# Dealing the MLP's products out between the small products of a chunked recurrence

## The chip, the cores and the metric

The kernel runs on one core of a Trainium2 chip. The metric is the device time of one execution in microseconds (us); lower is better. Five engines work side by side, each through its own instruction stream in order: TensorE (PE in the profile, PEld for its weight loads), VectorE (DVE), ScalarE (ACT), GpSimd (POOL) and the engine that issues transfers (SP). They wait for each other through semaphores. Products land in PSUM[...].

## The reference

Two stages. The first is a linear recurrence over 768 tokens for 4 batches of 8 heads, each with a 40x40 state:

```python
for t in range(S):
    y[:, :, t] = np.einsum('bhd,bhde->bhe', rt, state)
    Sa = np.einsum('bhde,bhe->bhd', state, at)
    state_decay = state * wt[:, :, None, :] - np.einsum('bhd,bhe->bhde', Sa, bt)
    state = state_decay + np.einsum('bhd,bhe->bhde', vt, kt)
```

The second is an MLP over the 3072 tokens, 320 to 1024 to 320 wide:

```python
h = x @ w_in
e = np.exp(h - h_max)
solu = h * (e / (np.sum(e) + 1e-09))
ln = (solu - mu) / np.sqrt(var + 1e-06) * g_ln
out = ln @ w_out
```

All is float32.

## The kernel before

**Tiling.** The sequence is cut into 12 chunks (rounds n) of 64 tokens. A step i handles one chunk for two of the four batches, so there are 24 steps, two to a round. Inside a step the recurrence becomes products of 64x64 blocks: two batches times eight heads make 16 products of 64x64 (or 64x40), issued as one group. Each of a group's 16 matmuls is float32 and appears in the profile as two records, so a group reads as x32. Full-size work stands beside it: transposes (four of 128x128 to a group) and the MLP, whose products are 128x512 (hidden layer `h`, six matmuls in two PSUM banks) and 128x320 (output `po`, eight matmuls in one bank).

**Parts.** Each piece of work is a Python generator that issues some instructions and yields; `turns` takes letters and resumes the part that a letter names.

- `front(i)` (f, g): logarithm of w (`lw`), its cumulated sums (`pcum`, `pcx`), scaled b and k on GpSimd, transposes of a and b, and the triangular matrix `nt`.
- `scatter`, `gather`: `nt` of a round goes through DRAM (`blk_dram`) to a layout with one matrix a partition (`blk`).
- `invert(n)` (I): a triangular inversion on VectorE of 30 pairs of small operations (L408, L410), an opening that waits for `blk` (L398) and a close (copy `ut` and stores to DRAM). `bring_inverse` loads the result back.
- `attend(i)` (a): transposes of k, v and r, score groups `psi` and `lamv`, then `px0`.
- `solve(i)` (s): two groups of 32x32 products, `py` and `pz`, that complete the inverse.
- `recurrence(i)` (r): decayed state `sm` (GpSimd, L513), `px`, `x0` (VectorE), `pu`, its transposes `psT` and `pnu`, the scores `lamu`, and the new state (`pst`, `tot`).
- `readout(i)` (y): `pyo` and the product with `exT`.
- `hidden(m)` (h) and `output(m)`: the MLP of step m = i - 6. `hidden` makes `h`, then the row maximum `nmax` (VectorE), `exp` into `e` (ScalarE), e times h in place (VectorE), and the statistics. `output` transposes the result (`plnT`, copied to `lnT` by ScalarE), multiplies by `w2` into `po`, and scales it into `osb` (ScalarE).
- `weights()` (W): narrows the MLP's weights piece by piece with VectorE, ScalarE and GpSimd (L163 to L174), and scales `w2` at its end (L238).

**Order.** The whole schedule is written by hand (`manual_schedule`): what the letters issue first stands first in each engine's queue. Steps 0, 1 to 5 and 6 to 23 use the strings FIRST, EARLY and STEADY (L684 to L686). After the string, a step calls `scatter`, the rest of the inversion (`steps(inv, ...)`), three weight pieces while i < 6, and in steady steps the whole of `output(m)`: eight transposes and eight products in a row (L740 to L741). In STEADY the products of `h` stand in two places: four of six matmuls behind `px` and `pcum`, two behind `pvT`. All small groups from `py` to `px0` follow one another. After step 23 a loop runs the last six `hidden` and `output` (L748 to L753).

**Buffers.** Small PSUM tiles of one bank (`bank`) rotate through two buffers, tiles of two banks (`duo`: all 64x64 groups) through two, and `h` has one of two banks. `e`, `lnT` and `osb` have one buffer each.

Of the kernel before, what the change touches and what calls it, by code (L numbers as in the profile page):

```python
# [17 lines left out]
P = 128  # L18
# [34 lines left out]
def kernel(  # L53
# [256 lines left out]
    def decay(i):  # L310
# [19 lines left out]
        for j in range(2):  # L330
            t = bank("pcx")
            for g in range(2):
# [3 lines left out]
                                 func=AF.Exp)  # L336

# [8 lines left out]
    def front(i):  # L346
# [8 lines left out]
        yield  # L355
        next(parts)
        yield
        next(parts, None)
# [76 lines left out]
    def attend(i):  # L435
# [6 lines left out]
        rT = d["rT"] = transposed("rT", given(i, "r"), "rT", 2)  # L442
        yield
        psi = d["psi"] = wide("psi")
        scores("psi", kT, d["aT"], psi)
        yield
# [59 lines left out]
    def recurrence(i):  # L506
# [15 lines left out]
        yield  # L522
        t = duo("pu")
# [13 lines left out]
        if ci:  # L537
            t = bank("psT")
            for c in range(2):
                for m in range(2):  # L540
                    at = (2 * c + m) * P
                    nc.tensor.transpose(out=t[:, at:at + P], in_=sm[:, c, 2 * m:2 * m + 2, :]
                                        .rearrange("q g d -> q (g d)"), identity=ident)
            sT = two.tile([P, 2, 2, P], FP32, tag="sT", name="sT", bufs=1)
            nc.scalar.copy(out=sT.rearrange("q c m e -> q (c m e)"), in_=t)
        yield
        t = bank("pnu")
        for g in range(G):
            nc.tensor.transpose(out=t[:, g * P:(g + 1) * P], in_=nuT[:, g, :], identity=ident)  # L549
        nc.scalar.copy(out=nu.rearrange("p h c -> p (h c)"), in_=t)  # L550
        yield
# [5 lines left out]
        scores("lamu", nuT, d["rT"], lamu)  # L557
        yield
# [49 lines left out]
    def hidden(i):  # L608
# [9 lines left out]
        part(0, 0)  # L618
        part(0, 1)
        yield  # L620
        part(1, 0)
        part(1, 1)
# [25 lines left out]
    def output(i):  # L648
# [7 lines left out]
        yield  # L656
        o = bank("po")
        for f in range(NF):
            nc.tensor.matmul(o[:, 0:DM], lhsT=lnT[:, f, :], rhs=w2[:, f, :], start=f == 0, stop=f == NF - 1)  # L659
        if s == 0:  # L660
            of_round[n]["osb"] = two.tile([P, 2, DM], FP32, tag="osb", name="osb", bufs=1)
        nc.scalar.activation(out=of_round[n]["osb"][:, s], in_=o[:, 0:DM], func=AF.Copy, scale=st[i]["rs"])  # L662
        yield
# [19 lines left out]

    FIRST = "r f r I a f a g a r r g f r f I s g y s I r a g a I f g a"  # L684
    EARLY = "r f I r a f a W a r r f r f I s W y s r W a a f a"
    STEADY = "r I f h r a f a h a r r h f r f s h y s r a a f a h h"  # L686
    front_of = {}

    def begin(i):
# [95 lines left out]
```

## Time and profile before

845.56 us, the median of 3 runs (839.35 to 847.56). The profiled execution spans 845.0 us.

| engine | busy us | share of the span | instructions |
|---|---|---|---|
| PE | 641.1 | 76% | 12281 |
| DVE | 462.4 | 55% | 1257 |
| ACT | 272.3 | 32% | 633 |
| POOL | 128.4 | 15% | 202 |

The costliest groups of instructions, with the mean time of one and the idle time of the engine just before them:

| line and operation | count | busy us | mean ns | idle before, us |
|---|---|---|---|---|
| L613 matmul h, 128x512 | 288 | 126.4 | 657 | 16.5 |
| L659 matmul po, 128x320 | 384 | 115.3 | 455 | 4.1 |
| L408, L410 inversion pairs on VectorE | 720 | 201.4 | 280 | 23.9 |
| L333 matmul pcx, 128x132 | 192 | 35.9 | 326 | 4.4 |
| L518 matmul px, 64x40 | 704 | 16.5 | 243 | 41.7 |
| L624 row maximum nmax | 24 | 29.4 | 1223 | 60.8 |

How to read them: a matmul counts as busy from its start to a modelled end, and neighbours overlap, so the rows for small groups show less than the time that they hold the engine. The idle column belongs to one engine; idle time of an engine that is not the bottleneck costs nothing. The `pu` groups, one to a step, mark the steps in time: step 0 begins at 64.5 us, step 1 at 102.4, step 6 at 268.5, step 19 at 642.7 and step 23 at 736.9.

### The profile page before, as it was taken

The numbers are of one execution on the slowest core, as the hardware profiler recorded it, in microseconds if no ns is written. First come the engines' busy times: TensorE is split into PE (matmuls) and PEld (weight loads), VectorE is DVE, ScalarE is ACT, GpSimd is POOL, SyncE is SP. The second block draws the span as 40 slices with busy tenths as digits, with TensorE's granted clock in tenths as the row PEclk, the third lists the DMA queues.
The fourth block names the chain that finished last, engine by engine and source line by source line (L and its number), as shares of the span: only waits on it lengthen the run. The fifth ranks groups of instructions, "written<-read, shape, count | busy, mean of one in ns | idle before, by whom it ended". The sixth has DMA issues, their size and how long they took to land.

```text
span 845.0 us, 28218 instructions
## 1 busy us (share of the span) xinstructions
PE 641.1 (76%) x12281; PEld 458.0 (54%) x12281; DVE 462.4 (55%) x1257; ACT 272.3 (32%) x633; POOL 128.4 (15%) x202
## 2 busy tenths in 40 slices
PE   5418365465477889888988988898888998978786
PEld 4316254354355666575667656665666666644344
DVE  2574375565538547467576585584675842342322
ACT  3113235344322333244234423432333332321211
POOL 3201124323301111111110111011110000000000
PEclk9659586696687998999899999999999999998988
DMA  7577445536504535425326346364213311010000
GB/s 113 92 126 114 120 89 111 122 61 108 108 1 82 94 56 88 86 50 99 75 58 90 67 78 108 66 99 78 50 31 75 76 36 44 5 35 0 16 16 16
DMA packets 269802, 59.99 MB, mean 71 GB/s; under 512 B 255464, under 2 KB 265328, under 8 KB 269680
## 3 DMA queue, kind: packets, MB, share of 16 engines
q1 hardware_dynamic: 269536, 57.98, 37.3%
q8 instruction: 96, 1.57, 0.8%
q10 hardware_dynamic: 144, 0.23, 0.1%
q14 instruction: 26, 0.21, 0.1%
HBM read 40.08 MB, written 13.37 MB: 63 GB/s over the span
## 4 chain that ended last, share of the span: by engine, by line
PE 51%; DVE 16%; issue 11%; ACT 6%; DMA 2%; POOL 1%; SPq 1%; ACTq 0%; DVEq 0%; POOLq 0%
PE h L613 11%; PE po L659 8%; DVE prod L408 4%; DVE u L410 4%; PE pyo L585 3%; PE pst L565 3%; PE plnT L654 2%; PE pcx L333 2%; DMA blk<-blk_dram 2%; PE pz L476 2%; PE pyo L502 2%; PE py L476 1%; PE pnu L549 1%; PE pu L529 1%; ACT rT L257 1%
## 5 line engine op out<-in xcount | busy, mean ns | idle before, releaser
L613 PE MATMUL h<-w_in,xT 128*128 128x512 f32 (+1 forms) x288 | 126.4, 657 | 16.5 <-DVE e L631 13.3
L659 PE MATMUL po<-w,lnT 128*128 128x320 f32 x384 | 115.3, 455 | 4.1 <-ACT lnT L655 4.1
L408 DVE TENSOR_TENSOR prod<-blk,u 128x30 f32<-128x30 f32 (+4 forms) x360 | 101.5, 282 | 11.5 <-DMA blk<-blk_dram 0.5
L410 DVE TENSOR_TENSOR u<-u,prod 128x30 f32<-128x30 f32 (+4 forms) x360 | 99.9, 278 | 12.4
L659 PEld LDWEIGHTS po<-w,lnT 128*128 128x128 f32 x384 | 75.0, 200 | 40.1 <-ACT lnT L655 8.8
L613 PEld LDWEIGHTS h<-w_in,xT 128*128 128x128 f32 (+1 forms) x288 | 42.7, 199 | 71.7 <-issue 71.4
L624 DVE TENSOR_REDUCE nmax<-h 128x1 f32<-128x1024 f32 x24 | 29.4, 1223 | 60.8 <-PE h L613 60.8
L572 POOL TENSOR_TENSOR st<-tot,kx 128x320 f32<-128x320 f32 x20 | 15.0, 749 | 282.0 <-DVE tot L571 282.0
L662 ACT ACTIVATE osb<-po,rs 128x320 f32<-128x320 f32 x24 | 12.7, 528 | 112.9 <-PE po L659 66.2
L518 PE MATMUL px<-sm,kx 64*64 64x40 f32 x704 | 16.5, 243 | 41.7 <-POOL sm L513 41.7
L631 DVE TENSOR_TENSOR e<-h,e 128x1024 f32<-128x1024 f32 x24 | 29.3, 1219 | 27.2 <-ACT e L628 27.2
L366 DVE TENSOR_TENSOR kx<-paT,kx 128x512 f32<-128x512 f32 x24 | 16.5, 690 | 48.7 <-PE paT L365 48.6
L646 POOL TENSOR_TENSOR rs<-c,mhalf 128x1 f32<-128x1 f32 x24 | 13.2, 549 | 193.7 <-DVE c L645 193.7
L518 PEld LDWEIGHTS px<-sm,kx 64*64 64x64 f32 x704 | 13.8, 149 | 49.8 <-POOL sm L513 42.2
L323 PE MATMUL pcum<-lw,cst 128*128 128x320 f32 x48 | 24.4, 597 | 21.5 <-ACT lw L319 21.5
L655 ACT COPY lnT<-plnT 128x512 f32<-128x512 f32 x48 | 26.3, 588 | 43.2 <-PE plnT L654 43.1
L534 ACT ACTIVATE nuT<-pu 128x128 f32<-128x128 f32 (+1 forms) x72 | 17.3, 313 | 70.4 <-PE pu L529 70.4
L460 ACT COPY x_own<-px 128x320 f32<-128x320 f32 x22 | 9.4, 426 | 94.0 <-PE px L454 94.0
L333 PE MATMUL pcx<-cst,lw 128*128 128x132 f32 x192 | 35.9, 326 | 4.4 <-ACT kT L257 4.2
L326 POOL TENSOR_TENSOR kx<-raw_b,inv 128x320 f32<-128x320 f32 x24 | 21.1, 880 | 97.1 <-ACT inv L324 84.0
L333 PEld LDWEIGHTS pcx<-cst,lw 128*128 128x128 f32 x192 | 30.4, 224 | 9.2 <-ACT kT L257 7.0
L520 DVE TENSOR_TENSOR x<-x_own,px 128x320 f32<-128x320 f32 x22 | 10.7, 486 | 43.1 <-PE px L518 26.1
(108 smaller groups left out, 1208.1 us busy)
## 6 DMA issues: line engine op xcount, KB each, us to landing
blk<-blk_dram SPq DMA_DIRECT2D x24, 256.0 KB
raw_w<-in_w_dram SPq DMA_DIRECT2D x24, 160.0 KB
raw_b<-in_b_dram SPq DMA_DIRECT2D x24, 160.0 KB
raw_a<-in_a_dram SPq DMA_DIRECT2D x24, 160.0 KB
raw_k<-in_k_dram SPq DMA_DIRECT2D x24, 160.0 KB
v<-in_v_dram SPq DMA_DIRECT2D x24, 160.0 KB
r<-in_r_dram SPq DMA_DIRECT2D x24, 160.0 KB
out_dram<-osb SPq DMA_DIRECT2D x24, 160.0 KB
```

Source lines behind the costliest of these rows:

```text
L333: nc.tensor.matmul(t[:, g * 132:g * 132 + 132], lhsT=pair(lw, 2 * j + g), rhs=cst[:, lo:lo + 132], start=True, stop=True)
L408: nc.vector.tensor_tensor(out=t, in0=nb[:, j:j + 1, j + 1:Q].to_broadcast([P, rows, m]), in1=u[:, 0:rows, j:j + 1].to_broadcast([P, rows, ...
L410: nc.vector.tensor_tensor(out=u[:, 0:rows, j + 1:Q], in0=u[:, 0:rows, j + 1:Q], in1=t, op=ALU.subtract)
L476: nc.tensor.matmul(t[quarter(out), c:c + Q], lhsT=lhs(p, g), rhs=rhs(p, g), start=True, stop=True)
L518: nc.tensor.matmul(t[half(c ^ p), p, g * D:g * D + D], lhsT=d["aT"][half(p), g, half(c)], rhs=sm[half(p), c, g, 0:D], start=True, stop=True)
L565: nc.tensor.matmul(t[half(p), c, g * D:g * D + D], lhsT=kb[half(c), j, 2 * g + p, :], rhs=x[half(c), G * p + g, 0:D], start=j == 0 and g = ...
L585: nc.tensor.matmul(t[half(p), c, g * L:g * L + L], lhsT=kb[half(c), j, 2 * g + p, :], rhs=lam[half(c), h % 2, h // 2, :], start=i < 2 and ...
L613: nc.tensor.matmul(h[:, j * 512:j * 512 + 512], lhsT=of_round[i // 2]["xT"][rows, kt, i % 2 * P:i % 2 * P + P], rhs=w_in[rows, 4 if kt == ...
L624: nc.vector.tensor_reduce(out=nmax, in_=h, axis=AX.X, op=ALU.max, negate=True)
L631: nc.vector.tensor_tensor(out=q, in0=h, in1=e, op=ALU.mult)
L655: nc.scalar.copy(out=lnT[:, fs.start:fs.stop].rearrange("p f t -> p (f t)"), in_=t)
L659: nc.tensor.matmul(o[:, 0:DM], lhsT=lnT[:, f, :], rhs=w2[:, f, :], start=f == 0, stop=f == NF - 1)
```

## The change

The MLP's large products are dealt out between the groups of small products, and the MLP of a step is spread over two steps. The intent is that large and small products alternate on TensorE, with less work standing in a clump.

- `hidden` makes `h` in five passes (both short products, then each of the other four alone) in place of two.
- `output` yields between its two groups of transposes and after each two of its eight products, and it runs one step later, dealt out by the letter o. The statistics of `hidden` (letter b) run one step later too. `store` moves into `output`.
- `decay` yields between the two `pcx` halves; `attend` makes `rT` after `psi`; in `recurrence`, `psT` comes before `pu`, and `pnu` after `lamu`.
- The three order strings are new. In EARLY (now also for step 0), five weight pieces are spread through the step, with none behind the string. The inversion has 12 steps in an early string and 16 in a steady one; what is left of it at the end of an even step is issued there, and now ahead of `scatter`.
- The loop after step 23 follows the new division.

```diff
@@ decay, front
                                  func=AF.Exp)
+            yield
...
-        next(parts)
-        yield
-        next(parts, None)
+        for _ in range(2):
+            next(parts)
+            yield
+        next(parts)
@@ attend
-        rT = d["rT"] = transposed("rT", given(i, "r"), "rT", 2)
-        yield
         psi = d["psi"] = wide("psi")
         scores("psi", kT, d["aT"], psi)
+        yield
+        rT = d["rT"] = transposed("rT", given(i, "r"), "rT", 2)
         yield
@@ recurrence: ahead of pu
+        if ci:
+            t = bank("psT")
...
+            nc.scalar.copy(out=sT.rearrange("q c m e -> q (c m e)"), in_=t)
+        yield
         t = duo("pu")
@@ recurrence: behind pu
-        if ci:
-            t = bank("psT")
...
-        t = bank("pnu")
-        for g in range(G):
-            nc.tensor.transpose(out=t[:, g * P:(g + 1) * P], in_=nuT[:, g, :], identity=ident)
-        nc.scalar.copy(out=nu.rearrange("p h c -> p (h c)"), in_=t)
-        yield
...
         scores("lamu", nuT, d["rT"], lamu)
+        yield
+        t = bank("pnu")
+        for g in range(G):
+            nc.tensor.transpose(out=t[:, g * P:(g + 1) * P], in_=nuT[:, g, :], identity=ident)
+        nc.scalar.copy(out=nu.rearrange("p h c -> p (h c)"), in_=t)
         yield
@@ hidden
-        part(0, 0)
-        part(0, 1)
-        yield
-        part(1, 0)
-        part(1, 1)
+        for j in range(2):
+            for kt in range(2):
+                yield
+                part(j, kt)
@@ output
-        yield
+            yield
         o = bank("po")
...
+            if f % 2 and f < NF - 1:
+                yield
...
+        if s:
+            store(n)
@@ the order
-    FIRST = "r f r I a f a g a r r g f r f I s g y s I r a g a I f g a"
-    EARLY = "r f I r a f a W a r r f r f I s W y s r W a a f a"
-    STEADY = "r I f h r a f a h a r r h f r f s h y s r a a f a h h"
+    EARLY = ("r r f I W r a r r I W y r a f I W a s a f W a f s f W a f",
+             "r r f g I W r a r r I W y r a f g I W a s a f g W a f g s f g W a f g")
+    STEADY = "r r f b b I r o o a o r r I o y o r I o a f h a s a h f I a h f s h f h a f h h"
@@ the loop over the steps
-            turns(FIRST if i == 0 else EARLY if i < LAG else STEADY,
-                  dict(I=4 if i < LAG else 6 if i % 2 else 12), **parts)
+            turns(EARLY[len(js) - 1] if i < LAG else STEADY, dict(I=4), **parts)
             if i % 2:
                 load((i + 3) // 2, "v", "r")
                 repack(i // 2)
+            else:
+                steps(inv, 99)
             if js and js[-1] % 2:
                 scatter(js[-1] // 2)
-            steps(inv, 9 if i % 2 else 99)
-            if i < LAG:
-                steps(ws, 3)
-            if m >= 0:
-                steps(output(m), 2)
-                if m % 2:
-                    store(m // 2)
             begin(i + 1)
+            after, before = now, output(m) if m >= 0 else None
@@ the loop behind step 23
-            turns("h o h o h h h h", {}, h=hidden(m), o=before)
...
+            turns("h h o o h h b b h o o o o h h", {}, h=now, b=after, o=before)
+            after, before = now, output(m)
+        turns("b b o o o o o o", {}, b=after, o=before)
```

## The prediction

> **What bounds the kernel now.** I read the page first, then the busy time by stretch, then the waits of two stretches, then timelines of TensorE, VectorE and ScalarE. From the page (sections 1, 2, 3 and 4):
>
> ```profile
> span 845.0 us, 28218 instructions
> PE 641.1 (76%) x12281; PEld 458.0 (54%) x12281; DVE 462.4 (55%) x1257; ACT 272.3 (32%) x633; POOL 128.4 (15%) x202
> PEclk9659586696687998999899999999999999998988
> q8 instruction: 96, 1.57, 0.8%
> PE 51%; DVE 16%; issue 11%; ACT 6%; DMA 2%; POOL 1%; SPq 1%; ACTq 0%; DVEq 0%; POOLq 0%
> ```
>
> TensorE is the fullest engine, but idle for 204 us, and 11% of the chain is "issue", time in which it waits for nothing that the profile shows. The stages differ, so I cut the span at the starts of the `pu` products (one per step): steps 0; 1 to 4; 7 to 18; 19 to 22; 23 with the tail. The columns are stretch, length, busy time of PE, PEld, DVE, ACT and POOL with counts, granted clock, DMA share, GB/s.
>
> ```profile
> 64.50:102.40 37.90, 19.55 (x470) 15.19 (x469) 16.64 (x53) 11.17 (x28) 5.21 (x7) 0.73 0.58 111
> 102.40:230.70 128.30, 71.97 (x1909) 59.62 (x1908) 76.09 (x236) 52.55 (x143) 42.08 (x67) 0.73 0.51 103
> 298.70:642.70 344.00, 301.64 (x6265) 217.18 (x6264) 220.51 (x578) 121.08 (x274) 47.25 (x69) 0.97 0.41 74
> 642.70:736.90 94.20, 84.48 (x1829) 59.84 (x1828) 47.70 (x120) 32.17 (x72) 7.22 (x11) 0.98 0.21 42
> 736.90:845.00 108.10, 82.20 (x413) 46.42 (x412) 31.16 (x58) 20.90 (x40) 3.84 (x7) 0.89 0.06 16
> ```
>
> Early steps 1 to 4 take 32.1 us each and no engine is busy for more than 19.1; steady steps take 28.7 us with TensorE busy for 25.1. So the early steps are bound by a wait and the steady ones by TensorE. The early wait, from the waits of 102.4 to 230.7:
>
> ```profile
> PE px L518 <- POOL sm L513: 41.7, 4, 12.1
> ACT parts L165 <- DVE parts L163: 34.2, 21, 5.4
> POOL w L174 <- DVE parts L171: 33.6, 12, 7.6
> ```
>
> At each step's end stand nine or more steps of the inversion on VectorE and then three weight pieces; their last operation is on GpSimd (L174), and the next step's `sm` (L513) queues behind it there. TensorE waits 10.4 us per step. In a steady step, from TensorE's timeline:
>
> ```profile
> 454.19 0.69 PE L585 MATMUL pyo<-lamu,kx 64*64 64x64 f32 x32
> ...
> 458.40 0.60 PE L565 MATMUL pst<-nu,kx 64*64 64x40 f32 x27 [1.48 <-issue]
> ...
> 460.78 1.13 PE L274 MATMUL pnt<-kx,bT 64*64 64x64 f32 x32
> ```
>
> The gap falls inside a group that has already begun, after seven small groups in a row, and afterwards such a group takes 1.13 us, not 0.69: the clock has dropped. The packets of the instruction queue tell why: 1.57 MB in 96 packets is 16.4 KB each, and in this step they start at 446.39, 455.20, 459.88 and 463.25 us, 3.4 to 4.7 us apart once the small groups run. Over steps 6 to 22 such gaps add up to 29 us of TensorE's idle time.
>
> **What the Trainium skill says.** "Runtime: NRT & Kernel Launch", Instruction fetch mechanics: each engine's instructions are refilled in 16 KiB blocks of 256, and the cost is mostly hidden. The trace agrees on the block (16.4 KB), not on hidden: the 12,281 matmuls and as many weight loads make 96 such blocks, and a small group (64 instructions in 0.5 to 0.7 us) uses a block in 2.4 us, faster than 3.4 to 4.7. "TensorE: Matmul & The Clock Gate", Part 1: idle time of about a window (3.4 us) halves the clock. Here 1.5 us was enough (0.69 to 1.13). "TensorEngine Tiling (Array Packing)", Key Properties: changing the tiling mode drains the engine. The trace has four transposes in 0.44 us where more transposes follow (449.70 to 450.14) and in 0.59 where a group of 32x32 follows (452.92 to 453.51), so some 0.1 us a change. "PSUM — Partial Sum Buffer", Engine vs sequencer instructions: ScalarE, VectorE and GpSimd are strict FIFOs; all waits above agree.
>
> **The change, part by part.** It adds no arithmetic; matmuls, copies and transfers are the same in number. Everything is order.
>
> Early steps. Weight pieces go from 3 in the step and 3 at its end to 5 spread through it; the inversion takes 12 steps in turn, and even steps still end with a clump of 8 (7 short pairs of some 0.45 us, as at 407.15 to 407.64, and the 0.61 copy: 3.75 us). `sm` no longer stands behind a weight piece that follows a clump: the 10.4 us wait goes. What stays is a chain on VectorE. An even step (0 is the end of `nt` of the step before): `x0` 1.3; `pu` 2.6 to 3.7; four pairs and a piece on VectorE to 5; `lamu` 6.1; four pairs, a piece, `x`, `tot` 10.5; four pairs, a piece, `psi` 14.4; a piece, `lamv`, `kx`, a piece 17.4; then `bT`, `pnt`, `nt` 19.1 us. An odd step meets a new wait: the scatter now stands behind the clump and its stores: 3.75 + 1.7 (issue of the stores) + 1.8 (of four scatters) + 2.0 (landing, as from 43.71 to the gather at 45.74) + 3.8 (gather to VectorE's start: 3.6 to 4.2 in the trace) = 13.1 us, and VectorE stops at its first inversion step after `x0` (4.2) until then. Behind it stand 1.4 us of setup (416.04 to 417.43), three pairs 1.4 (417.43 to 418.83), a piece 0.8 and `lamu` 0.7 = 17.4; TensorE's `pyo` and all after it wait. The remaining 12.2 us are VectorE's, as in the even step: 29.6 us. Two pairs are 2 x (19.1 + 29.6) = 97.4, against 128.3: **minus 31**. Bounds: 27 us instead of 29.6 if the gather is early, 24 instead of 19.1 if GpSimd or the clock drags: minus 21 to minus 36. Step 5 (mean product, 6.3 us, in both): minus 1. Step 0: the gain-row product `pg` now stands before `pu` and waits for GpSimd to free the round's inputs, some 9 us, where 7.24 us were waited at the step's end; 5.87 us of waiting for `lw` go: minus 4, between plus 5 and minus 10.
>
> Steady steps. The densest stretches are now px0, pnt, px, psT, pcum, pu (280 instructions in some 5 us) and pyo to ppsi, in which 9 large products stand between the groups (about 256 in 5.2 us): slower than the fetch, so the "issue" gaps (29 us in steps 6 to 22, 1.7 a step) go, and with them the lost clock (3% of 25.1, 0.7 us). Mode changes rise from 11 to about 17: plus 0.4. Busy: 25.1 - 0.7 + 0.4 = 24.8. New waits, from 0 at the end of h's last pass: `nmax` 1.28, `exp` 2.5, its product 3.76 and `x0` 4.25, since VectorE runs `e` before `x0`; TensorE has px0, pnt, px, psT and pcum (3.0 us; pcum itself waits for `lw`, behind `exp` on ScalarE, to 3.0), so `pu` waits 1.3. pkT needs the bank of the first transposes, freed by ScalarE at 6.4: 0.45 with po. pcx needs po's bank, freed by `osb`: 0.25. Sum 26.8 on even steps. The 0.2 to 0.5 us waits for `lw`, `kT`, `rT` and `lnT` of before are replaced by these. On odd steps VectorE's queue has the gather's wait in it:
>
> ```profile
> 404.70 0.69 DVE L276 TENSOR_TENSOR nt<-pnt,cst 128x512 f32<-128x512 f32 x1 [0.40 <-PE pnt L274]
> ...
> 412.75 0.49 DVE L520 TENSOR_TENSOR x<-x_own,px 128x320 f32<-128x320 f32 x1 [2.43 <-ACT osb L662]
> 416.04 0.42 DVE L398 TENSOR_SCALAR u<-blk 64x512 f32<-64x512 f32 x1 [2.80 <-DMA blk<-blk_dram]
> ```
>
> Today that wait is hidden: `lamu` is needed 12 us after `px`, behind two stretches of h. After the change `nt` ends at 2.0, the data are there 2.0 + 4.3 + 3.8 = 10.1, setup, three pairs and `lamu` follow to 13.6, and `pyo` could have run at 10.6: plus 3.0 (1.5 to 5, and a cold clock may add 1). So 29.8, and a pair averages 28.3 against 28.7: **minus 5** for steps 7 to 18, from minus 30 (no new waits) to plus 25. Step 6 has no output product yet (5.6 us) and loses a 4.5 us wait, against 1.6 new: minus 8.5. Steps 19 to 22: 0, the same exchange.
>
> Tail. One more output product stands in step 23 and the exponent's chain there is bare: plus 9. The period of the last six stays: po's four parts still stand before the exponent, so on ScalarE
>
> ```profile
> 770.06 0.53 ACT L662 ACTIVATE osb<-po,rs 128x320 f32<-128x320 f32 x1 [5.46 <-issue]
> 770.49 1.11 ACT L628 ACTIVATE e<-h,nmax 128x1024 f32<-128x1024 f32 x1
> ```
>
> `osb`, which waits for po, still precedes `exp`, and TensorE's 3.2 us idle follows, with h at 4.69 instead of 3.04 us.
>
> Sum: -4 - 31 - 1 - 8.5 - 5 + 9 = -40.5: 845.5 to about 805; I say **806**.
>
> **Rivals.** (B) The gather lands early or the waits for `x0` and `lamu` overlap, and the steady stage keeps the whole of issue gaps and clock: 12 x 2.4 more = 29 less: **777**. For it: the gaps are real, and step 9 shows only 24.2 us of TensorE work (27.03 less 2.8 idle). Against: `lamu` follows `px` so soon now. (C) The early steps gain only 15, because the clump and its stores hold the gather longer, and odd steady steps wait 5 us: **840**, no change to speak of. (D) Slower: each steady step pays for `x0` and `lamu` in full and the idle time drops the clock (1.7 us each, as in the tail), 31.0 a step: plus 28, tail plus 9, early minus 20: **862**. For it: three strict queues are now chained in each step. Against: VectorE is busy for 18 of 28.7 us only.
>
> **How the numbers follow.** A 0.50 (790 to 825), B 0.25, C 0.11, D 0.14. Faster by over 1%: A, B and a little of C: 0.77; same 0.09; slower 0.14. The range 766 to 846 leaves out some of B's lower end and most of D.
>
> **What would show it.** Right: `px <- POOL sm` gone from the early waits, early pairs near 49 us; issue gaps in steady steps below 0.5 us; new rows `pu <- DVE x`, `pyo <- DVE lamu` (odd steps), `pcum <- ACT lw` near 1 us; tail unchanged. Wrong: issue gaps still there (then fetch is not what they are), `sm` still late, or a clock under 0.95 in the steady stage.

## The result, and the profile after

894.7 us (median of 4 runs, 891.7 to 899.8) against 846.6 for the kernel before beside it: ratio 1.059, 95% interval 1.050 to 1.068. Forecast were 806 us, with 766 to 846 as range. The change makes the kernel slower, by 48 us. The profiled execution (899.8 us) is the longest of the four.

The page's lines that answer to those shown of before (sections 1, 2, 3 and 4):

```profile
span 898.0 us, 28194 instructions
PE 663.6 (74%) x12281; PEld 464.5 (52%) x12281; DVE 464.2 (52%) x1257; ACT 272.1 (30%) x633; POOL 127.1 (14%) x202
PEclk9655758657656998999999999999999999887978
q8 instruction: 97, 1.59, 0.8%
PE 51%; DVE 16%; SPq 10%; DMA 9%; ACT 7%; issue 6%; POOL 0%; ACTq 0%; DVEq 0%; POOLq 0%
```

The arithmetic is the same (12,281 matmuls), but TensorE is busy for 22.5 us more on it. "issue" fell from 11% of the chain to 6%, as meant; but SyncE's queue went from 1% to 10% and the transfers from 2% to 9%. PEclk shows where: in slices 2 to 13 there are five fives and no nine, where the kernel before had two of each, and five of the last six are below nine again.

By the same stages, again cut at the starts of `pu` (step 0; 1 to 4; 7 to 18; 19 to 22; 23 with the tail):

```profile
82.90:107.50 24.60, 21.96 (x469) 18.30 (x469) 13.70 (x37) 12.27 (x32) 4.73 (x7) 0.68 0.19 63
107.50:256.80 149.30, 76.76 (x1915) 64.19 (x1914) 80.28 (x246) 47.97 (x133) 38.93 (x62) 0.69 0.39 79
326.80:671.00 344.20, 305.29 (x6264) 211.82 (x6264) 218.71 (x583) 122.02 (x274) 47.12 (x69) 0.97 0.42 77
671.00:772.20 101.20, 86.76 (x1826) 58.54 (x1826) 48.28 (x121) 32.55 (x72) 7.20 (x11) 0.96 0.22 43
772.20:898.00 125.80, 98.17 (x440) 55.18 (x440) 32.96 (x64) 22.40 (x42) 4.38 (x8) 0.83 0.06 14
```

| stage | before | after | difference | predicted |
|---|---|---|---|---|
| up to step 0's `pu` | 64.5 | 82.9 | +18.4 | |
| step 0 | 37.9 | 24.6 | -13.3 | with the row above: -4 |
| steps 1 to 4 | 128.3 | 149.3 | +21.0 | -31 |
| step 5 | 37.8 | 45.8 | +8.0 | -1 |
| step 6 | 30.2 | 24.2 | -6.0 | -8.5 |
| steps 7 to 18 | 344.0 | 344.2 | +0.2 | -5 |
| steps 19 to 22 | 94.2 | 101.2 | +7.0 | 0 |
| step 23, tail | 108.1 | 125.8 | +17.7 | +9 |

The early steps (up to step 6, plus 34) and the end (from step 19 on, plus 25) make it slower, not the steady steps. The waits of steps 1 to 4, first TensorE's, then VectorE's, then the fullest of ScalarE's (that one from 107.5 to 302.6, step 5 included); columns: who waits, for what, us in total, times, longest:

```profile
PE plamu L274 <- ACT nuT L546: 38.2, 4, 20.4
PE pbT L255 <- ACT tinvT L493: 14.0, 2, 7.5
PE pcx L333 <- ACT y_mid L490: 8.9, 4, 2.9
...
DVE parts L163 <- DMA bits<-in_moe_w_out_dram: 19.4, 2, 9.7
DVE u L400 <- DMA blk<-blk_dram: 18.2, 2, 9.2
...
ACT parts L165 <- DVE parts L163: 89.4, 16, 19.6
```

`px <- POOL sm` is gone, as predicted. But of the 72 us that TensorE now waits in these steps, 62 are for copies by ScalarE, and ScalarE stands in a weight piece (L165) for VectorE's part of it (L163), which stands behind either the gather of the inversion's blocks (`u`, odd steps) or the piece's own bits (even steps). (Not all inputs are float32: the two weight matrices of the MLP arrive as 64-bit numbers, `bits`, and a piece narrows a stretch of them.) Step 1 in order of time, on VectorE, ScalarE and TensorE:

```profile
124.65 0.42 DVE L400 TENSOR_SCALAR u<-blk 64x512 f32<-64x512 f32 x1 [9.17 <-DMA blk<-blk_dram]
127.40 0.29 DVE L163 TENSOR_SCALAR parts<-bits 128x256 int32<-128x256 int32 x1
127.73 0.51 ACT L165 ACTIVATE parts<-parts,ebias 128x256 int32<-128x256 int32 x1 [19.65 <-DVE parts L163]
128.77 0.70 ACT L546 ACTIVATE nuT<-pu 128x256 f32<-128x256 f32 x3
129.18 1.13 PE L274 MATMUL plamu<-rT,nuT 64*64 64x64 f32 x32 [20.37 <-ACT nuT L546]
```

One late transfer holds VectorE, VectorE holds ScalarE, ScalarE holds `nuT`, and TensorE idles 20.4 us; its next group takes 1.13 us, at a granted clock of 0.50. In step 2 it is SyncE's queue, a line of transfers to issue from 145.26 on (its first row and its last two), before VectorE's wait for bits that came last in it:

```profile
145.26 2.27 SPq L300 DMA_DIRECT2D v<-in_v_dram  x2
...
168.22 2.72 SPq L300 DMA_DIRECT2D raw_k<-in_k_dram  x2
171.05 6.50 SPq L213 DMA_DIRECT2D bits<-in_moe_w_out_dram  x5
...
174.78 0.24 DVE L163 TENSOR_SCALAR parts<-bits 128x160 int32<-128x160 int32 x1 [9.72 <-DMA bits<-in_moe_w_out_dram]
```

The Trainium skill ("Perfetto Trace Analysis", DMA Instruction — HWDGE (DVE, Sync)) says that a queue's sequencer is free for the next instruction only when the descriptors of the last are made. The trace agrees: 35 issues follow one another from 145.26 to 172.60, 0.78 us each on average and at most 0.11 us apart, and the first of the weights' fetches stood behind 32 of them. (The last row runs to 177.55 because its last two fetches wait, for 4.1 us together, until VectorE frees their buffers.)

The steady steps did what was predicted, but for step 7. TensorE's waits from 326.8 to 671:

```profile
PE pyo L587 <- DVE lamu L276: 18.1, 6, 5.1
PE pu L541 <- DVE x L522: 10.7, 13, 3.6
PE pcum L323 <- ACT lw L319: 4.5, 11, 0.4
...
PE pst L567 <- issue: 0.4, 1, 0.4
```

No gap for instructions is left (0.4 us in twelve steps), even steps take 26.4 (step 8: 27.1), odd ones 28.2 to 31.7, and step 7 takes 34.9.

### The profile page after: what moved, and what is told of

The parts are those of the page before. It is cut to its first block, busy times and chain, and to the rows that moved or that the text cites. A ratio compares the mean times of both kernels' runs of the same rounds, so it can differ in the third digit from the quotient of the medians.

```text
span 898.0 us, 28194 instructions
## 1 busy us (share of the span) xinstructions
PE 663.6 (74%) x12281; PEld 464.5 (52%) x12281; DVE 464.2 (52%) x1257; ACT 272.1 (30%) x633; POOL 127.1 (14%) x202
## 4 chain that ended last, share of the span: by engine, by line
PE 51%; DVE 16%; SPq 10%; DMA 9%; ACT 7%; issue 6%; POOL 0%; ACTq 0%; DVEq 0%; POOLq 0%
PE h L615 13%; PE po L660 10%; DMA blk<-blk_dram 4%; SPq L300 4%; DVE u L412 3%; DVE prod L410 3%; PE pyo L587 3%; PE pcx L333 3%; DVE nmax L625 2%; PE pst L567 2%; DMA blk_dram<-nt 2%; SPq L385 2%; ACT e L629 2%; DVE e L632 2%; PE plnT L655 2%
## 5 line engine op out<-in xcount | busy, mean ns | idle before, releaser
L615 PE MATMUL h<-w_in,xT 128*128 128x512 f32 (+1 forms) x288 | 137.1, 682 | 19.6 <-DVE e L632 16.5
L660 PE MATMUL po<-w,lnT 128*128 128x320 f32 x384 | 129.0, 471 | 0.1
L412 DVE TENSOR_TENSOR u<-u,prod 128x30 f32<-128x30 f32 (+4 forms) x360 | 109.0, 303 | 12.4
L274 PE MATMUL plamu<-rT,nuT 64*64 64x64 f32 x768 | 18.2, 241 | 48.8 <-ACT nuT L546 48.8
L333 PE MATMUL pcx<-cst,lw 128*128 128x132 f32 x192 | 34.6, 313 | 15.3 <-ACT y_mid L490 10.8
L333 PEld LDWEIGHTS pcx<-cst,lw 128*128 128x128 f32 x192 | 29.4, 212 | 27.0 <-ACT y_mid L490 15.9
L276 DVE TENSOR_TENSOR lamu<-plamu,cst 128x512 f32<-128x512 f32 x24 | 16.5, 689 | 50.3 <-PE plamu L274 50.3
L400 DVE TENSOR_SCALAR u<-blk 64x512 f32<-64x512 f32 x12 | 5.2, 431 | 71.9 <-DMA blk<-blk_dram 67.5
L541 PE MATMUL pu<-tinvT,x 64*64 64x64 f32 x768 | 20.2, 246 | 29.8 <-DVE x L522 19.4
L274 PEld LDWEIGHTS plamu<-rT,nuT 64*64 64x64 f32 x768 | 15.6, 153 | 50.0 <-ACT nuT L546 50.0
L647 POOL TENSOR_TENSOR rs<-c,mhalf 128x1 f32<-128x1 f32 x24 | 13.1, 548 | 194.6 <-DVE c L646 180.7
L165 ACT ACTIVATE parts<-parts,ebias 128x160 int32<-128x160 int32 (+1 forms) x26 | 11.9, 458 | 92.6 <-DVE parts L163 92.6
L656 ACT COPY lnT<-plnT 128x512 f32<-128x512 f32 x48 | 26.9, 603 | 41.7 <-PE plnT L655 41.6
L541 PEld LDWEIGHTS pu<-tinvT,x 64*64 64x64 f32 x768 | 16.8, 150 | 39.9 <-DVE x L522 27.3
```

The costliest lines, as they stand in the source:

```text
L274: nc.tensor.matmul(t[half(c ^ p * cross), p, g * L:(g + 1) * L], lhsT=lhs[half(p), g, half(c)], rhs=rhs[half(p), g, half(c)], start=True, ...
L333: nc.tensor.matmul(t[:, g * 132:g * 132 + 132], lhsT=pair(lw, 2 * j + g), rhs=cst[:, lo:lo + 132], start=True, stop=True)
L412: nc.vector.tensor_tensor(out=u[:, 0:rows, j + 1:Q], in0=u[:, 0:rows, j + 1:Q], in1=t, op=ALU.subtract)
L541: nc.tensor.matmul(t[half(z), c ^ p, h // 2 * L:h // 2 * L + L], lhsT=x0[half(c ^ p), h, :], rhs=d["tinvT"][half(c ^ p), p, h % G, :], sta ...
L615: nc.tensor.matmul(h[:, j * 512:j * 512 + 512], lhsT=of_round[i // 2]["xT"][rows, kt, i % 2 * P:i % 2 * P + P], rhs=w_in[rows, 4 if kt == ...
L656: nc.scalar.copy(out=lnT[:, fs.start:fs.stop].rearrange("p f t -> p (f t)"), in_=t)
```

## The experiments

All ratios are to the kernel before, with 95% intervals; "steps 1 to 4" is the time between the starts of `pu` in steps 1 and 5. It is read from one profiled execution of each kernel; kernels that have the same early steps agree in it within 1.5 us (149.3, 149.1 and 148.5; 134.0, 133.8 and 135.0; 128.3 and 127.2), so differences of 3 us or less say little.

**Which stages lose.** Two edits, each to the changed kernel: the early steps dealt out as before (`OLD` holds the strings of before, fitted to the new parts), and the tail's exponent ahead of the output product.

```diff
-            turns(EARLY[len(js) - 1] if i < LAG else STEADY, dict(I=4), **parts)
+            turns(OLD[len(js) - 1] if i < LAG else STEADY, dict(I=4), **parts)
...
-            else:
-                steps(inv, 99)
             if js and js[-1] % 2:
                 scatter(js[-1] // 2)
+            if i < LAG:
+                steps(inv, 9 if i % 2 else 99)
+                steps(ws, 3)
+            elif i % 2 == 0:
+                steps(inv, 99)
```

> Steps 0 to 5 run in the order of the kernel before (its strings, its clump of the inversion, three weight pieces at the step's end, scatter ahead of the clump); everything else is the changed kernel, the new order of psT, pnu and rT included. Theory A (the early strings are the loss): step 6 begins near 268 us as in the kernel before and not at 302.6, and the whole takes about 860 (855 to 868). Theory B (the new order of the parts themselves, psT ahead of pu and rT behind psi, costs the early steps): step 6 begins after 285 and the whole stays above 875.

849.2 us, ratio 1.005 (1.002 to 1.008): 46 us less, Theory A and more than it said; step 6 begins at 264.3. Steps 1 to 4 take 134.0 and wait for `sm` again (40.9 us), step 5, whose mean product moved into step 4, 24.2. Steps 7 to 18 take 334.1, 9.9 less than before. The edit does more there than its expectation says: in steady steps, too, the scatter stands ahead of the inversion's rest. Step 7, 34.9 in the changed kernel, takes 28.1 (below, the scatter's place alone gives 28.6).

```diff
-            turns("h h o o h h b b h o o o o h h", {}, h=now, b=after, o=before)
+            turns("h h o o h h b b h h o o o o h", {}, h=now, b=after, o=before)
```

> In the loop behind step 23 the exponent is issued ahead of the four parts of the output product, so that on ScalarE it no longer stands behind osb; nothing else. Theory A (the order of osb and exp on ScalarE makes the 3.1 us idle time of each round and the low clock after it): the round falls from 15.4 to about 10.5 us, six rounds, so 25 to 30 us less, about 867. Theory B (the maximum, exponent and product chain is longer than the output product anyway): 5 us less or nothing.

862.0 us, ratio 1.019 (1.013 to 1.026): Theory A. Step 23 and the tail fall from 125.8 to 92.0. ScalarE in a round of the changed kernel, then in one of this:

```profile
805.52 0.53 ACT L665 ACTIVATE osb<-po,rs 128x320 f32<-128x320 f32 x1 [6.47 <-PE po L660]
805.95 1.11 ACT L629 ACTIVATE e<-h,nmax 128x1024 f32<-128x1024 f32 x1
```

```profile
808.54 1.11 ACT L629 ACTIVATE e<-h,nmax 128x1024 f32<-128x1024 f32 x1 [3.15 <-DVE nmax L625]
...
811.71 0.53 ACT L665 ACTIVATE osb<-po,rs 128x320 f32<-128x320 f32 x1 [1.97 <-issue]
```

In the first `exp` waits behind `osb`, which waits for the whole of `po`; in the second it runs while TensorE computes `po`, and a round takes 9.9 us instead of 15.4 on average. The edit works on the kernel before as well:

```diff
-            turns("h o h o h h h h", {}, h=hidden(m), o=before)
+            turns("h o h h o h h h", {}, h=hidden(m), o=before)
```

> The kernel before with one edit in the tail: the exponent stands ahead of the output product and its osb. Theory A (the tail's idle 3.2 us a round and the cold clock after it are the kernel's own, not the change's, and five rounds each lose 4 to 5 us): 846 less 22 = 824 us (818 to 830). Rival B (the gain needs the four parts of the output product that the change made): less than 8 us, 838 to 847 us.

819.6 us, ratio 0.972 (0.963 to 0.981), the tail 84.0 for 108.1. So the idle time in a round is the kernel's own; the swap shortens five rounds here and six in the changed kernel. And the two losses add:

> The changed kernel with both edits that gained by themselves: steps 0 to 5 dealt out as before, and in the tail the exponent ahead of the output product's last parts. Theory A (the two losses lie in different stages and add): 849 less 34 = 815 us (808 to 822), step 6 begins near 264, the tail from the start of step 23 takes 92. Rival B (the tail's gain came out of work that the late early steps had pushed on): the tail gains 15 at most, 834 us (827 to 845).

817.1 us, ratio 0.964 (0.959 to 0.968), step 6 at 265.3.

**What the early steps lose to.** First with all weights ahead of the loop, so that no piece stands in the steps:

```diff
         ws, after, before = weights(), None, None
+        steps(ws, 99)
```

> All weight pieces are worked off ahead of step 0, so that none stands in the early strings; the whole is not comparable, the early steps are. Theory A (a weight piece's ScalarE part stands ahead of the recurrence's copies and hands VectorE's wait on to TensorE): the waits plamu on nuT, pbT on tinvT and pcx on y_mid fall under 1 us a step, and steps 1 to 4 take 95 to 110 us together in place of 149. Theory B (the gather blocks VectorE and lamu behind it, weights or not): odd steps stay at 33 us or more and TensorE waits over 10 us for lamu in each; only the even ones fall, to about 22, so steps 1 to 4 take 110 to 125.

877.1 us (a single run; the pieces' time is now ahead of step 0, which begins at 130.4). The stretch of steps 1 to 4, and TensorE's wait in it:

```profile
151.40:256.10 104.70, 62.96 (x1913) 52.84 (x1912) 65.25 (x186) 30.50 (x73) 15.37 (x21) 0.82 0.44 80
```

```profile
PE pyo L587 <- DVE lamu L276: 28.8, 4, 18.2
```

The sum, 104.7 us or 44.6 less, is Theory A's, and what is left is Theory B's: behind the gather TensorE waits for `lamu` 18.2 us in step 1 and 8.8 in step 3, where it had waited 20.4 and 10.6 for `nuT`. So in odd steps the late gather makes most of that wait, pieces or not; ScalarE's queue only gives it another name. Even steps fall from 37.7 and 37.1 to 21.1 and 20.8, odd ones from 41.2 and 33.3 to 35.5 and 27.4: some 16 us of an even step and 6 of an odd one are the pieces'. (The kernel before has pieces in these steps too; what its steps would take without them was not measured.) What of a piece costs that? Three edits to its place and that of its transfers:

```diff
-    EARLY = ("r r f I W r a r r I W y r a f I W a s a f W a f s f W a f",
+    EARLY = ("r r f r a r r I W I W y r a f I W a s a f W a f s f W a f",   # and so in step 0's string
```

> The changed kernel with one edit in the strings of steps 0 to 5: the first weight piece of a step, and the four inversion steps ahead of it, stand behind the recurrence's pu, nuT and lamu rather than ahead of pu. As many pieces as before. Theory A (TensorE waits because ScalarE's and VectorE's queues hold the weight piece, and with it the gather, ahead of nuT and lamu): the 48.8 us of waiting for nuT fall below 10, steps 1 to 5 take 150 to 165 instead of 195, the time is 860 us (850 to 870). Rival B (what paces these steps is the SP queue, which issues loads, scatters, stores and weights in one line: the weights' bits come when they come): the wait moves to y_mid, tinvT and the copies after them, steps 1 to 5 stay at 185 to 195, 885 to 895 us.

882.6 us, ratio 1.041 (1.036 to 1.046); steps 1 to 4 146.3 (of the 12 us gained, 7.8 are gained ahead of step 1, for step 0's pieces moved too). Rival B in effect, though the wait went elsewhere than it said:

```profile
PE ppsi L274 <- DVE x L594: 28.9, 4, 12.0
PE pbT L255 <- ACT tinvT L493: 11.4, 2, 5.8
```

None for `nuT` is left; 28.9 are for the readout's `x`, next in VectorE's queue. So `y` and the rest of the recurrence were put ahead of the pieces too (again in place of the change's string):

```diff
+    EARLY = ("r r f r a r r y r a I W I W f I W a s a f W a f s f W a f",   # and so in step 0's string
```

> The changed kernel with, in steps 0 to 5, the whole recurrence and readout of the step ahead of its first inversion steps and weight pieces: where moving them behind lamu alone had pushed the wait for the gather from nuT to the readout's x, x stands ahead of it too. Theory A (the odd steps' loss is VectorE's wait for the gather, ahead of whatever TensorE needs next): odd steps fall from 41.2, 33.3 and 45.8 to 30 to 34 each, even ones little; 872 us (862 to 880). Rival B (the wait moves once more, to psi, the next that VectorE must give): odd steps stay within 3 us of 41.9, 32.5 and 43.5, 880 to 890 us.

886.7 us, ratio 1.050 (1.043 to 1.057), steps 1 to 4 147.4: Rival B's total, but the wait did not go to `psi`, which it had named:

```profile
PE prT L255 <- ACT kx L335: 22.6, 4, 7.0
PE pcx L333 <- ACT y_mid L490: 11.9, 4, 3.4
PE py L478 <- DMA tinv<-ut_dram: 10.6, 4, 6.6
```

Moving a piece alone moves the wait. Next, the lines that make VectorE late: the weights' fetches from GpSimd's queue,

```diff
-                nc.sync.dma_start(out=to[row:row + part.shape[0]], in_=part)
+                nc.gpsimd.dma_start(out=to[row:row + part.shape[0]], in_=part)
```

> The changed kernel with the weights' fetches (bits) issued from GpSimd's queue and not SyncE's; all else as it is. Theory A (even early steps are long because bits are issued behind loads, repacking and stores in SyncE's one line): VectorE's 19.4 us of waiting for bits go, even steps 2 and 4 fall from 37.7 and 37.1 to 24 to 28, step 6 begins at 265 to 280 and not 302.6, 865 us (855 to 875). Rival B (the line is full either way, and what counts is the coupling of ScalarE's queue to VectorE's): even steps stay above 34, 885 to 900 us. Rival C (issue from GpSimd costs GpSimd more than it saves): sm and the pieces' last operation come later, above 900 us.

885.7 us, ratio 1.048 (1.041 to 1.055). The mechanism is A's: the wait for bits is gone and the even steps fall to 29.1 and 29.3 (A said 24 to 28), steps 1 to 4 to 133.6. The time is B's: the odd steps stay (42.1, 33.0, 45.7), and the profiled execution, 880.4, is the fastest of four. Then the scatter ahead of the inversion's rest, and the gather with it:

```diff
-            else:
-                steps(inv, 99)
             if js and js[-1] % 2:
                 scatter(js[-1] // 2)
+                gather(js[-1] // 2)        # only in the second kernel; taken from the next step's top
+            if i % 2 == 0:
+                steps(inv, 99)
```

> At the end of an even step the scatter is issued ahead of the rest of the inversion and its stores, as in the kernel before; nothing else. Theory A (the late gather is what odd early steps wait for): the gather of steps 1, 3 and 5 lands 4 to 6 us sooner and the whole falls by 12 to 18 us, to about 880. Theory B (the transfer engine's own queue, full of stores, loads and fetches, is the limit, or the gather still waits for the stores): 0 to 5 us.

876.9 us, ratio 1.037 (1.030 to 1.045), Theory A's time, though `u` starts only 3.2 to 3.5 us sooner after `nt` and not 4 to 6; steps 1 to 4 141.1, steps 7 to 18 334.1, step 7 28.6 (34.9). SyncE and VectorE at the start of step 7, in the changed kernel and in this one:

```profile
326.41 0.35 SPq L418 DMA_DIRECT2D ut_dram<-ut  x1
328.19 2.45 SPq L385 DMA_DIRECT2D blk_dram<-nt  x4
...
336.05 0.42 DVE L400 TENSOR_SCALAR u<-blk 64x512 f32<-64x512 f32 x1 [7.42 <-DMA blk<-blk_dram]
```

```profile
308.39 1.92 SPq L385 DMA_DIRECT2D blk_dram<-nt  x4
313.36 0.34 SPq L418 DMA_DIRECT2D ut_dram<-ut  x1
...
318.98 0.42 DVE L400 TENSOR_SCALAR u<-blk 64x512 f32<-64x512 f32 x1 [3.40 <-DMA blk<-blk_dram]
```

In step 7 of the changed kernel the gather is late for the same reason as in odd early steps: the scatter stands behind the inversion's rest and its stores, and `u` starts 14.6 us after `nt`, here 10.6. Step 7 is the last to suffer from it, since a string of step 5 and one of step 6 issue 12 + 16 of the inversion's 32 steps, and two steady ones all 32. It is no backlog of the early steps: with the weights ahead step 7 takes 35.6. The gather moved as well:

> The changed kernel with the scatter and the gather of the inversion's blocks both ahead of the inversion's rest at the end of an even step (the gather stood at the top of the next step, in SyncE's line behind the stores of that rest). Theory A (the loss of odd steps, early and steady, is the gather's landing, 17.1 us after nt in step 1): the landing comes 8 to 10 us after nt, steps 1, 3 and 5 fall from 41.2, 33.3 and 45.8 to 32, 27 and 37, the odd steady steps to 26.5, and 895 less 45 = 850 us (840 to 862). Rival B (the scatter's place alone did what the gather can do, and what is left of the odd steps is ScalarE behind the weight piece): as with the scatter ahead alone, 872 to 880 us, odd steps at 38, 29 and 42.

880.0 us, ratio 1.036 (1.029 to 1.043), steps 1 to 4 139.9: Rival B's figures. VectorE's wait says why the earlier gather brought no more:

```profile
118.20 0.42 DVE L400 TENSOR_SCALAR u<-blk 64x512 f32<-64x512 f32 x1 [3.88 <-DMA u_dram<-u]
```

The blocks are there, but `u` has one buffer, and the last inversion's store of it has not landed: 11.8 us after `nt` (17.1 in the changed kernel), one limit in place of another. In the steady steps `pyo` waits for `lamu` 13.7 us instead of 18.1. Both lines mended:

> As the kernel with scatter and gather ahead of the inversion's rest, and the weights' fetches issued from GpSimd's queue as well. Theory A (two causes, one in odd steps and one in even steps, and both are places in SyncE's line): even steps at 29 or less, odd ones at 27 to 33, steps 1 to 4 together 105 to 120 (149.3 after, 128.3 before, 97.4 by the prediction); 834 us (820 to 846). Rival B (with the lines mended VectorE's and ScalarE's queues still hold the pieces in a chain, so one mend takes the other's gain): steps 1 to 4 above 125, 846 us or more.

869.9 us, ratio 1.026 (1.020 to 1.031), steps 1 to 4 128.5: Rival B, though most of the two gains is kept (9.4 and 15.7 singly, 20.8 together); 29.3 us of waiting for `nuT` are left. Now the piece's place was tried again, with two buffers for `u`:

```diff
-        u = two.tile([P, Q // 2, Q], FP32, tag="u", name="u", bufs=1)
+        u = two.tile([P, Q // 2, Q], FP32, tag="u", name="u", bufs=2)
...
+    EARLY = ("r r f r a r r I W y r I W a f I W a s a f W a f s f W a f",   # and so in step 0's string
```

> As the kernel with scatter and gather ahead of the inversion's rest and the weights fetched from GpSimd's queue, and two more edits: two buffers for the inversion's u (with one, the next inversion waited 3.9 us for the store of the last), and in steps 0 to 5 the first inversion steps and weight piece behind lamu, the second behind the readout's x. Theory A (what was left in steps 1 to 4, 128.5 us, is the queues' order: nuT on ScalarE behind the piece that stands behind the inversion on VectorE; moving the piece pays now that the gather no longer stops VectorE): the 29 us of waiting for nuT in these steps fall below 5, steps 1 to 4 take 105 to 114 together, 852 us (845 to 860). Rival B (the weights' own chain through three engines is what bounds them, wherever the pieces stand): steps 1 to 4 stay above 120, 862 us or more.

850.7 us, ratio 1.008 (1.005 to 1.011). The waits for `nuT` are gone, and this time the time follows, to A's 852; but steps 1 to 4 take 120.3, at the edge of B. TensorE's waits in them, and the busy times of the four steps together:

```profile
PE py L478 <- ACT vT L257: 16.0, 4, 4.7
PE pcx L333 <- ACT y_mid L490: 9.1, 4, 3.5
```

```profile
sum 120.30, PE 74.64 PEld 61.40 DVE 84.36 ACT 48.10 POOL 51.07; mean PE 18.66 PEld 15.35 DVE 21.09 ACT 12.02 POOL 12.77
```

The kernel with the weights ahead takes 15.6 us less (104.7), though its gather is as late as the change's. Its even steps are 10 us shorter (21.1 and 20.8 against 30.9 and 31.0), its odd ones longer (35.5 and 27.4 against 32.1 and 26.3). Of the 15.6 us, 11.7 are TensorE's busy time on the same products (74.64 against 62.96 us; granted clock 0.64 to 0.79 in the four steps against 0.82 over all). TensorE's waits are now for other copies of ScalarE, which still serves the pieces; that the pieces cause them was not tested, nor whether another order would take them away.

The four steps of each of these kernels, in us, in the order of their sums:

| kernel | step 1 | step 2 | step 3 | step 4 | sum |
|---|---|---|---|---|---|
| changed | 41.2 | 37.7 | 33.3 | 37.1 | 149.3 |
| readout ahead of the pieces | 40.5 | 38.7 | 30.0 | 38.2 | 147.4 |
| first piece behind `lamu` | 41.9 | 35.9 | 32.5 | 35.9 | 146.3 |
| scatter first | 37.9 | 36.7 | 29.3 | 37.1 | 141.1 |
| scatter and gather first | 35.8 | 37.8 | 29.7 | 36.6 | 139.9 |
| fetches from GpSimd's queue | 42.1 | 29.1 | 33.0 | 29.3 | 133.6 |
| both: scatter and gather first, fetches from GpSimd's queue | 37.0 | 30.3 | 29.8 | 31.4 | 128.5 |
| before | 34.4 | 31.9 | 31.3 | 30.8 | 128.3 |
| the same two, with two buffers for `u` and the pieces later | 32.1 | 30.9 | 26.3 | 31.0 | 120.3 |
| all pieces ahead of step 0 | 35.5 | 21.1 | 27.4 | 20.8 | 104.7 |

**Step 0, steady steps, and the best.** The gain row and the first fetches ahead of the loop:

```diff
         ws, after, before = weights(), None, None
+        steps(ws, 1)
```

> The changed kernel with the fetch of the gain row, its product pg and the first weight fetches ahead of step 0 and so ahead of the fourth round's loads in the SP queue. Theory A (the row's transfer stood behind loads that wait for the round's inputs to come free): TensorE's wait ahead of pg goes from 16.7 us to 2 to 4, step 0 begins at 68 to 71 instead of 82.9, and what was won stays won: 881 us (876 to 886). Rival B (the gain is given back at the first gather, which comes when its data are there): step 1 ends where it ended, 891 to 898 us.

884.7 us, ratio 1.045 (1.039 to 1.052): Theory A's time, though the wait ahead of `pg` is still 7.9 us (16.7 in the changed kernel) and not 2 to 4. Step 0 begins at 72.9, 10 us earlier, and it stays won.

```diff
-    STEADY = "r r f b b I r o o a o r r I o y o r I o a f h a s a h f I a h f s h f h a f h h"
+    STEADY = "r r f b b r o o a o r I r I o y o r I o a f h a s a h f I a h f s h f h a f h h"
```

This edit (the inversion's first steps behind `lamu` and not ahead of it), with the scatter first, the gain row, the pieces behind `lamu` and the tail:

> The changed kernel with its own dealing in all steps and every mend at once: weight pieces behind lamu in steps 0 to 5, gain row first, scatter ahead of the inversion's rest, in steady steps the first four inversion steps behind lamu rather than ahead of it, exponent first in the tail. Theory A (each loss has its own cause and the mends add): step 0 begins at 70, step 6 at 250 (235 to 262), odd steady steps take 26.9 instead of 28.2 to 31.7 and the wait of pyo for lamu falls below 1 us a step, tail 92: 785 us (765 to 805). Rival B (spreading the weights through the early steps can't be as fast as the clumps of before, since each piece chains three engines): step 6 begins at 265 to 285, 805 to 830 us. Rival C (the wait for lamu in odd steps is not for the gather but for what stands behind it): odd steady steps stay at 28 or more.

811.7 us, ratio 0.957 (0.952 to 0.962). Odd steady steps from step 9 on take 26.4, as the even ones, and no wait for `lamu` is left: it was the inversion's start, which waits for the gather and stood ahead of `lamu` in VectorE's queue, and Rival C falls. (The edit by itself: the next kernel differs in it alone from the one with the early steps as before and the exponent first, and takes 317.5 for steps 7 to 18 instead of 336.3.) Step 6 begins at 272.6, by Rival B. So the best of each:

> Steps 0 to 5 dealt out as before, steady steps with the first four inversion steps behind lamu, exponent first in the tail. Theory A (the parts add: 817 us with the first and the third, less 17 that steps 7 to 18 took less with the second, less 4 in steps 19 to 22): 796 us (789 to 803), all steady steps at 26.4. Rival B (the time won in odd steps is lost where the inversion's rest then ends later, in the clump of even steps and the stores behind it): 806 to 816 us, even steps longer than 26.4.

797.9 us, ratio 0.945 (0.939 to 0.952), Theory A. The strings of before up to step 5, then the change's with the two edits. Steps 7 to 18:

```profile
287.30:604.80 317.50, 296.15 (x6264) 206.00 (x6264) 217.67 (x583) 121.92 (x274) 48.87 (x71) 1.00 0.44 82
```

26.5 us a step at full clock, TensorE busy for 93%. The change's own early strings, first with the gather, the fetches, the gain row and the tail mended, then with everything:

> As the kernel before this one in the list, with the gain row and the first fetches ahead of step 0 and the exponent first in the tail; the strings of all steps are the change's own. Theory A (all three losses that are not the strings' own are mended, so the change's dealing gives what it can): 834 less 34 less 10 = 790 us (775 to 800), steps 1 to 4 105 to 120, all steady steps 26.4 to 27, tail 92. Rival B (the early gain is given back in step 5 or 6, since the weights' last product then waits): 805 to 825 us.

824.4 us, ratio 0.972 (0.967 to 0.977): Rival B's figure, but not its reason. Theory A started from 834 for the kernel without the last two mends, which took 869.9; the two gain what it said they would. Steps 1 to 4 take 127.2 and odd steady steps 28.2 to 31.4, for this kernel has neither the edit to the steady string nor that of the pieces' place.

> As the kernel before this one in the list, with the gain row ahead of step 0, the first inversion steps of a steady step behind lamu and the exponent first in the tail. Theory A (all losses mended, the dealing of the change kept): 852 less 34 (tail), less 19 (steps 7 to 18, 337 to 318), less 10 (step 0) = 789 us (778 to 797), below the 798 of the kernel with the early steps as before. Rival B (early steps stay above 120): 797 to 812 us.

794.3 us, ratio 0.943 (0.938 to 0.948): Theory A's time, with steps 1 to 4 at 121.8, which was Rival B's. Its interval overlaps that of the kernel with the early strings of before (0.939 to 0.952), so which of the two is faster is not shown.

## Why the prediction was wrong

**What failed: "minus 31" for steps 1 to 4 (plus 21 came).** The step that failed is the price of a weight piece, "a piece 0.8" of VectorE's time. VectorE's share was right: its five pieces are 3.9 us of step 2 (busy for 21.0 us against 17.2 with the pieces ahead). But a piece is a chain, VectorE, ScalarE, VectorE, GpSimd, on bits that SyncE's line must fetch, and its ScalarE part stands ahead of TensorE's copies. The prediction saw GpSimd's queue (`sm`) and not ScalarE's: it took one 10.4 us wait away and asked only VectorE what would take its place. Counted as it counts, from the end of one `nt` to that of the next, in us:

| | predicted | less five pieces of 0.8 | measured | measured with the pieces ahead |
|---|---|---|---|---|
| even steps (2, 4) | 19.1 | 15.1 | 33.5, 32.4 | 16.2, 15.8 |
| odd steps (1, 3) | 29.6 | 25.6 | 39.4, 38.0 | 34.6, 32.2 |

(In an even step the first of the five pieces may lie beside `pu`; then 15.9 stands for 15.1.) The four steps exceed the 97.4 by 46.0. Of these, some 28 are pieces (44.5 in place of 16.0) and some 18 the chain without them, nearly all in odd steps. That the kernel with the pieces ahead comes near 97.4 (104.7 by the cut at `pu`) is luck in part, for the 97.4 hold 16 us of pieces.

**The even step's chain on VectorE: right** but for the pieces, within 1.1 us. Moving the fetches took some 8 us of the 16 to 17 back (37.7 to 29.1, 37.1 to 29.3); for the other half no single cause is shown.

**The gather, "13.1 us after `nt`".** 17.1 in step 1, 14.9 in step 3. The clump was mis-sized: from the end of `nt` to the store of `ut` passed 7.9 and 5.5 us, not 3.75. `lamu` then ended 6.4 us after VectorE's start, not 4.3; with the pieces ahead it was 3.4, so the piece between them costs 3.0. From there to `nt` 12.2 us were counted, pieces included; it took 15.9 and 16.8, and 13.9 and 13.3 without pieces, at a granted clock of 0.71 and 0.74 in these steps (0.94 and 1.00 in the even ones). The direction was right, and the early landing named as a bound (27 us a step) never came.

**Step 0, "minus 4".** Plus 5. The wait for `pg` was seen at some 9 us and measured 16.7; it stood ahead of step 0's `pu`, so it counted in full.

**Steady steps, "minus 5": the mechanism was right, and the size but for step 7.** Even steps 26.4 (26.8 predicted), odd ones from step 9 on 28.2 to 31.7 (29.8). The issue gaps went; in the even steps the granted clock was 1.00 and TensorE busy for 24.7 us (24.8 predicted; 25.0 in step 8, 23.9 in step 18); `pu <- DVE x`, `pyo <- DVE lamu` and `pcum <- ACT lw` appeared as named. The wait for `lamu` came to 18.1 us in six odd steps, 3.0 each as predicted, though 5.1 of it fell in step 7; that for `x0` was 0.5 in the other steps where 1.3 was said. That the stage shows plus 0.2 is step 7, for whose late gather nothing was counted: its granted clock was 0.85, and the stage's 0.97 as before. Rival B (all of 29 us) had the size that is there once `lamu` is freed: 317.5 is 26.5 less than before.

One reading of the clock in the prediction is too simple. A gap of 1.48 us (at 458.40) was followed by half the clock, but in the same trace gaps of 1.64 and 1.81 us (at 514.39 and 630.75) were passed at full clock. The length of one gap does not decide it; what does is not shown here.

**Steps 19 to 22, "0".** Plus 7.0. The exchange isn't the same: `pu` waits 2.6 us in each. The view names nothing that ended the wait, but in step 21 `x0` stands behind `e` on VectorE until 723.64 and `pu` begins at 723.74. No later front is left whose `pcum` and `pcx` would fill that time.

**Tail, "plus 9".** Plus 17.7. From the start of `pu` in step 23 to the first `exp` pass 17.8 us instead of 4.1, since all of that step's `h` and the output product of the step before are still to come: 13.7 of the 17.7 us, where only the output product and a bare chain had been counted. The six rounds after it are 0.7 us longer each. That "the period stays" was nearly right (15.4 against 14.7), and so was the line that shows why; that it could be shortened by a swap was not asked.

Rival D forecast slower (862), but by steady steps of 31.0, which did not come.

## What to carry to other kernels

When filler work is moved between dependent products, follow each filler through every queue that it touches, its fetch among them: in a queue that is served in order it puts the latest thing it waits for ahead of all that stands behind it. Moving a piece back by one place moved the wait to the next product (3.0 us gained in four steps); what paid was an earlier arrival of its data and of the gather (20.8), and after that its place together with a second buffer (8.2). A chain that stays bare (the tail's exponent) deserves its own account whatever the change is about: one swap of two letters gave 24 us in the kernel before and 34 in the changed one.

## What the runs showed of the hardware

- Back to back, 35 issues on SyncE took 0.78 us each on average (0.36 to 1.99). A fetch of a 128x160 weight piece took 0.33 to 0.60 us to issue there in step 2, and 0.58 from GpSimd. What moving the fetches gained was the place in the line and not a cheaper issue.
- Idle time is paid twice. The same products of steps 1 to 4 kept TensorE busy for 76.8 us in the changed kernel, where it idles for 72.5 of 149.3 us at a granted clock of 0.69, and for 63.0 with the weights ahead (idle for 41.7 of 104.7, clock 0.82). But the sum of the idle time does not set the clock alone: with two buffers for `u` and the pieces later it idles for 45.7 of 120.3 us, a smaller share, at a clock of 0.72. With the weights ahead, 27.0 of the 41.7 us are two waits for `lamu`; in the other kernel no wait is longer than 6.1.
